# Long convolution and cosine-gated MLP: evictions shared out anew, matrices of two steps made by ScalarE and GpSimd, some made a step earlier

## The chip, the cores and the metric

The kernel runs on one core of a Trainium2 chip. The metric is the device time of one execution in microseconds (us), where lower is better. Kernels are compared by fast runs, and all runs of this study were fast. A difference under 2% counts as "same". All differences here but one (e11) are below that mark, so I give 95% intervals.

PE is TensorE's matmuls, PEld its weight loads, DVE VectorE, ACT ScalarE, POOL GpSimd, SP (or SPq) SyncE, which issues the transfers. An eviction is the copy of a matmul's result out of PSUM (where the matmuls of this kernel write) into SBUF (where its other tiles lie).

## The reference

```
# x, v: (4, 12480, 128)
h_filt = relu(pos_emb @ w1) @ w2 * exp(-0.01 * pos)      # the filter
y = irfft(rfft(x*v, 2S) * rfft(h_filt, 2S))[:S]          # long convolution
z = (x * y).reshape(49920, 128)
h = z @ w_in                                             # 128 -> 2048
out = (h * cos(h)) @ w_out                               # 2048 -> 128
```

## The kernel before

The convolution is done as a transform in two factors (96 and 120) with matmuls. For batch 0 the stages come one after the other: u = x·v and the filter, the **first step** (of the filter, then of the data), the **second step** with the product in frequency, the **third step**, and the **last step**, which runs beside the first blocks of the MLP. The matrices of the second step (w) and the last step (tm) are made on the chip for batch 0 and stored in DRAM; the other batches load them. All later convolution work is interleaved with the MLP.

Every such matrix is a sum of two scaled rows. This helper makes one:

```
def turn(dst, first, second, one, other, half=None, spare=None):
    term = dst
    if half is not None:
        term = half()[...]                       # a PSUM bank
    nc.scalar.activation(term, first, AF.Copy, scale=one)              # ScalarE
    if spare is None:
        nc.vector.scalar_tensor_tensor(out=dst, in0=second, scalar=other, in1=term,
                                       op0=ALU.mult, op1=ALU.add)      # VectorE
    else:
        nc.gpsimd.tensor_scalar(out=spare, in0=second, scalar1=other, ...)
        nc.gpsimd.tensor_tensor(dst, term, spare, op=ALU.add)
```

The second step (48 iterations, two matrices each) has two buffers for w and for h, both stored by SyncE in program order (h is the filter after its second step):

```
with tc.tile_pool(name="both", bufs=2) as pool:
    def before(j):
        ws[j] = pool.tile([KE, 2, N2], F32, name="w")
        for i in range(2):
            make_w(ws[j][:, i, :], 2 * j + i, half=bank)
        nc.sync.dma_start(wd[j, :, :, :], ws[j][:, :, :])
    ...
    def after(j, ps):
        h = pool.tile([N2, 2, 2, D], F32, name="h")
        nc.scalar.activation(h..., ps[1][0:N2, :], AF.Copy, scale=1.0 / M)
        nc.sync.dma_start(hd[j, :, :, :, :], h[:, :, :, :])
        yield from f2_product(pool, ps[0], h, 2 * j)   # VectorE products, GpSimd sums
```

The last step of batch 0 makes four matrices for each of 30 groups, three by VectorE and one by GpSimd, with one spare buffer (`bufs=1`). Beside it run the u multiplies and sums of batch 1, and the MLP, whose step per 128 hidden features is this chain over four engines:

```
ph = w_in.T @ at                      # PE
a  = ph / (2 pi) + 0.25               # ScalarE
k  = (a + ROUND) - ROUND              # VectorE
f  = a - k                            # GpSimd
cs = sin(2 pi f)                      # ScalarE, one step later
gt = ph * cs                          # VectorE
acc += w_out.T @ gt                   # PE
```

## Time and profile before

The median is 3817.88 us over four runs (3814.89 to 3822.04). The profiled execution has a span of 3819.3 us.

| engine | busy share of the span |
|---|---|
| PE | 97% |
| VectorE | 73% |
| GpSimd | 67% |
| ScalarE | 65% |

These shares average a long stretch in which PE is full with a short beginning in which it isn't. Only the beginning can give something back. The borders of its stages are marks in the trace: the first matmul of a step, the first transposes of the MLP, and the 30 results "zs" of the last step.

| stage of batch 0 | us before |
|---|---|
| u, filter, first steps: until the second step's first matmul | 182.4 |
| second step | 106.6 (its h instructions 2.14 apart) |
| third step | 59.8 |
| start of the last step, until the MLP's first transposes | 19.4 |
| from there to the last zs, 617.6 | 249.4 (its zs 9.07 apart) |

### The profile page before, as it was taken

What the parts mean: (1) busy time and instruction counts of PE and PEld (TensorE: products, weight loads), DVE (VectorE), ACT (ScalarE), POOL (GpSimd) and SP (SyncE); (2) the same over time, 40 slices, a digit from 0 to 9 for tenths busy, and PEclk for the clock granted to TensorE, in tenths of its full rate; (3) what the DMA queues carried; (4) which work ended last, traced back from release to release, by engine and by line L of the source; (5) the groups of instructions that cost most, each with busy time, mean ns of one, the idle gap of its engine ahead of it and who ended that gap; (6) DMA issues with size and microseconds to landing.
All of it is one profiled execution on the core that took longest, in us unless ns stands there. A gap on an engine that the chain in (4) does not pass through costs nothing.

```text
span 3819.3 us, 47226 instructions
## 1 busy us (share of the span) xinstructions
PE 3713.3 (97%) x13546; PEld 2117.3 (55%) x13546; DVE 2804.5 (73%) x5737; ACT 2488.4 (65%) x4597; POOL 2559.8 (67%) x2307
## 2 busy tenths in 40 slices
PE   7797989999999999999999999999999999999999
PEld 6777545655566555545566556555566544444444
DVE  7796898678876787787766787787765566666666
ACT  5654666766665556766655567666664677777777
POOL 6564776478854665588845664788644577777776
PEclk9898999999999999999999999999999999999999
DMA  6163442022201651122203640222105200000000
GB/s 164 49 174 93 134 144 79 12 72 78 77 25 29 188 175 30 31 75 78 68 12 96 182 131 12 57 75 77 49 18 164 83 17 22 18 17 23 17 17 17
DMA packets 209082, 274.65 MB, mean 72 GB/s; under 512 B 17062, under 2 KB 146486, under 8 KB 208694
## 3 DMA queue, kind: packets, MB, share of 16 engines
q1 hardware_dynamic: 208822, 271.63, 24.5%
q8 instruction: 109, 1.79, 0.2%
q14 instruction: 151, 1.24, 0.1%
HBM read 191.93 MB, written 79.63 MB: 71 GB/s over the span
## 4 chain that ended last, share of the span: by engine, by line
PE 85%; DVE 5%; POOL 3%; DMA 3%; ACT 2%; issue 2%; SPq 0%; DVEq 0%; POOLq 0%; ACTq 0%
PE ph L691 32%; PE acc L716 28%; PE cv L716 5%; PE cv L482 5%; PE cv L457 4%; PE cv L394 3%; PE cv L433 3%; PE ph L126 2%; POOL f L700 2%; DMA hd<-h 2%; PE ps L457 1%; ACT cs L705 1%; DVE k L697 1%; PE ps L394 1%; DVE xt L382 1%
## 5 line engine op out<-in xcount | busy, mean ns | idle before, releaser
L700 POOL TENSOR_TENSOR f<-a,k 128x512 f32<-128x512 f32 x1568 | 1989.4, 1269 | 1070.6 <-DVE k L697 1067.8
L691 PE MATMUL ph<-at,w_in_sb 128*128 128x512 f32 x3136 | 1602.7, 592 | 18.6 <-DVE gt L707 18.2
L694 ACT ACTIVATE a<-ph,quarter 128x512 f32<-128x512 f32 x1568 | 1073.3, 684 | 756.9 <-PE ph L691 747.8
L716 PE MATMUL acc<-gt,w_out_sb 128*128 128x512 f32 x2656 | 1362.4, 594 | 5.5 <-ACT ot L722 5.3
L707 DVE TENSOR_TENSOR gt<-ph,cs 128x512 f32<-128x512 f32 x1568 | 1078.1, 688 | 326.4 <-ACT cs L705 298.2
L697 DVE TENSOR_SCALAR k<-a 128x512 f32<-128x512 f32 x1568 | 781.5, 498 | 599.4 <-ACT a L694 583.6
L705 ACT ACTIVATE cs<-f 128x512 f32<-128x512 f32 x1568 | 980.3, 625 | 363.8 <-POOL f L700 362.2
L716 PEld LDWEIGHTS acc<-gt,w_out_sb 128*128 128x128 f32 x2656 | 500.9, 189 | 651.2 <-issue 614.1
L691 PEld LDWEIGHTS ph<-at,w_in_sb 128*128 128x128 f32 x3136 | 553.9, 190 | 358.3 <-issue 262.9
L452 POOL TENSOR_TENSOR slots<-slots,t 120x256 f32<-120x256 f32 x384 | 310.9, 816 | 63.0 <-DVE t L451 25.8
L482 PEld LDWEIGHTS cv<-slots,tm 96*104 96x104 f32 x1920 | 243.0, 172 | 100.0 <-issue 86.0
L482 PE MATMUL cv<-slots,tm 96*104 96x128 f32 x1920 | 254.6, 275 | 3.8 <-DVE tm L282 3.8
L716 PE MATMUL cv<-gt,w_out_sb 128*128 128x512 f32 (+1 forms) x480 | 238.5, 579 | 1.0 <-DVE gt L707 1.0
L457 PEld LDWEIGHTS cv<-cs,slots 120*96 120x96 f32 x1536 | 176.9, 167 | 69.1 <-issue 68.7
L457 PE MATMUL cv<-cs,slots 120*96 120x120 f32 x1536 | 183.2, 266 | 0.0
L433 PE MATMUL cv<-slots,w 124*120 124x256 f32 x576 | 173.0, 380 | 0.0
L433 PEld LDWEIGHTS cv<-slots,w 124*120 124x120 f32 x576 | 103.3, 184 | 122.4 <-issue 109.4
L394 PEld LDWEIGHTS cv<-c,slots 104*124 104x124 f32 x768 | 132.8, 192 | 63.8 <-issue 58.3
L716 PEld LDWEIGHTS cv<-gt,w_out_sb 128*128 128x128 f32 x480 | 90.9, 190 | 110.2 <-issue 106.9
L394 PE MATMUL cv<-c,slots 104*124 104x192 f32 x768 | 150.4, 326 | 0.0
L382 DVE TENSOR_TENSOR xt<-xt,vt 104x256 f32<-104x256 f32 x200 | 143.0, 717 | 0.7 <-DMA vt<-in_v_dram 0.4
L467 DVE TENSOR_TENSOR slots<-cv,other 96x240 f32<-96x240 f32 x384 | 133.6, 394 | 2.8 <-ACT other L465 2.8
(125 smaller groups left out, 2529.3 us busy)
## 6 DMA issues: line engine op xcount, KB each, us to landing
h<-hd SPq DMA_DIRECT2D x144, 240.0 KB
tm<-td SPq DMA_DIRECT2D x90, 312.0 KB
xt<-in_x_dram SPq DMA_DIRECT2D x120, 208.0 KB
vt<-in_v_dram SPq DMA_DIRECT2D x120, 208.0 KB
xs<-in_x_dram SPq DMA_DIRECT2D x120, 208.0 KB
zd<-zs SPq DMA_DIRECT2D x120, 208.0 KB
zb<-zd SPq DMA_DIRECT2D x97, 256.0 KB
w<-wd SPq DMA_DIRECT2D x144, 116.2 KB
```

Source lines behind the costliest of these rows:

```text
L394: nc.tensor.matmul(ps[0:KE, i * 2 * N1:(i + 1) * 2 * N1], u[:, b, 0:KE, i], c1[0:u.shape[0], :, :].rearrange("p r k -> p (r k)"), start=Tr ...
L433: nc.tensor.matmul(pi, w[:, i, :], parts[0:KE, :, k], start=True, stop=True)
L452: nc.gpsimd.tensor_tensor(y[:, r], y[:, r], t[:, r], op=op)
L457: nc.tensor.matmul(ps[0:N1, (i * 2 + r) * N2:(i * 2 + r + 1) * N2], parts[0:N2, r, :, b, i], cs[:, r, :], start=True, stop=True)
L482: nc.tensor.matmul(ps[0:R, i * D:(i + 1) * D], t[:, i, r, :], slots[0:N1, :, place, :], start=(r == 0), stop=(r == 1))
L691: nc.tensor.matmul(ph[:, 0:m], w_in_sb[:, c * P:(c + 1) * P], ats[n][:, 0:m], start=True, stop=True)
L694: nc.scalar.activation(a[:, 0:m], ph[:, 0:m], AF.Identity, bias=quarter[:, 0:1], scale=INV_TWO_PI)
L697: nc.vector.tensor_scalar(out=k[:, 0:m], in0=a[:, 0:m], scalar1=ROUND, scalar2=ROUND, op0=ALU.add, op1=ALU.subtract)
L700: nc.gpsimd.tensor_tensor(f[:, 0:m], a[:, 0:m], k[:, 0:m], op=ALU.subtract)
L705: nc.scalar.activation(cs[:, 0:m], f[:, 0:m], AF.Sin, scale=TWO_PI)
L707: nc.vector.tensor_tensor(gt[:, 0:m], ph[:, 0:m], cs[:, 0:m], op=ALU.mult)
L716: nc.tensor.matmul(accs[n][:, 0:m], w_out_sb[:, c, :], gt[:, 0:m], start=(c == 0), stop=(c == NFC - 1))
```

## The change

The intent is to take work from VectorE where it is the busiest engine. The first steps give more evictions to ScalarE. In the second step one of the two w of an iteration is made by ScalarE (two scalings) and GpSimd (an add). In the last step two of four matrices are made so, 15 u multiplies go to GpSimd, and six of the 30 groups are made beside the third step and only loaded later. The essential parts of the diff:

```diff
     def turn(...)
-            nc.gpsimd.tensor_scalar(out=spare, in0=second, scalar1=other, scalar2=None,
-                                    op0=ALU.mult)
+            nc.scalar.activation(spare, second, AF.Copy, scale=other)
             nc.gpsimd.tensor_tensor(dst, term, spare, op=ALU.add)
 ... (F1 evictions: f1_takers(b) -> f1_takers(b, share), the share to ScalarE)
-        if b % 2 == 0:
+        if int((b + 1) * share) > int(b * share):
 ... (second step)
-                for i in range(2):
-                    make_w(ws[j][:, i, :], 2 * j + i, half=bank)
+                make_w(ws[j][:, 0, :], 2 * j, half=bank)
+                spare = pool.tile([KE, N2], F32, name="spare")
+                make_w(ws[j][:, 1, :], 2 * j + 1, spare=spare[:, :])
 ... (last step)
+    SOME = range(4, NG, 5)
+    def make_group(pool, g, t, summed, bufs=1):     # `summed` matrices by ScalarE + GpSimd
+        for i, n2 in enumerate(n2s(g)):
+            if i < G - summed:
+                make_t(t[:, i, :, :], n2)
+            else:
+                spare = pool.tile([N1, 2, R], F32, name="spare", bufs=bufs)
+                make_t(t[:, i, :, :], n2, spare=spare[:, :, :])
+            yield
+        nc.sync.dma_start(td[g, :, :, :, :], t[:, :, :, :])
-                if b == 0:
-                    ... (three matrices by VectorE, one with a spare, bufs=1)
+                if b == 0 and j not in SOME:
+                    for _ in make_group(pool, j, ts[j], G // 2):
+                        pass
                 else:
                     nc.sync.dma_start(ts[j][:, :, :, :], td[j, :, :, :, :])
 ... (u of batch 1)
-        new = u_units(b + 1, 3, slots[0:R, :, :, :], lambda j, half: nc.vector,
+        new = u_units(b + 1, 3, slots[0:R, :, :, :],
+                      lambda j, half: nc.gpsimd if b == 0 and j % 2 > half else nc.vector,
 ... (8 u multiplies of batch 0 also to GpSimd; shares 0.53 and 0.57 for the first steps;
      the inverse tables' sines one table later; 3.4 -> 3.5 MLP steps per group in the last step;
      SOME's groups made beside the third step)
```

More of the change, by code (lines that the diff above doesn't have):

```diff
@@ L182, with __init__ @@
     class Tables:
-        def __init__(self, pool, engine):
+        def __init__(self, pool, engine, lag):
             self.pool, self.engine = pool, engine
+            self.lag, self.waiting = lag, []
             self.prod, self.moved = (
@@ L205, in sines @@
             for dst, quarters in outs:
-                turned = self.pool.tile([P, P], F32, name="turned", bufs=2)
+                turned = self.pool.tile([P, P], F32, name="turned", bufs=self.lag + 1)
                 m, t = self.moved[0:p, 0:n], turned[0:p, 0:n]
@@ L217, in sines, with finish @@
                 self.engine.tensor_tensor(t, m, t, op=ALU.subtract)
+                self.waiting.append((dst, t, TWO_PI / turn))
                 yield
-                nc.scalar.activation(dst, t, AF.Sin, scale=TWO_PI / turn)
+                if len(self.waiting) == self.lag:
+                    self.finish(1)
+        def finish(self, n):
+            for _ in range(n):
+                dst, t, scale = self.waiting.pop(0)
+                nc.scalar.activation(dst, t, AF.Sin, scale=scale)
     def forward_tables(pool):
-        t = Tables(pool, nc.vector)
+        t = Tables(pool, nc.vector, 1)
         part = t.whole([P, 1], [[1, 1]], channel_multiplier=1, name="part")
@@ L245, in inverse_tables @@
     def inverse_tables(pool):
-        t = Tables(pool, nc.gpsimd)
+        t = Tables(pool, nc.gpsimd, 2)
         part = t.whole([P, 1], [[1, 1]], channel_multiplier=1, name="part")
@@ L260, in inverse_tables @@
                            eighths=slice(H - 1, N2, H))
+        t.finish(1)
         for kept, made in ((csd, cs), (rowsd, rows), (twd, tw_t)):
@@ L396, in f1_mm, with f1_takers @@
                          start=True, stop=True)
-    def f1_takers(b):
-        if b % 2 == 0:
+    def f1_takers(b, share):
+        if int((b + 1) * share) > int(b * share):
             return nc.scalar.copy, lambda out, in_: nc.scalar.activation(
@@ L404, in f1_takers, with f1_evict @@
             out=out, in0=in_, scalar1=-1.0, scalar2=None, op0=ALU.mult)
-    def f1_evict(ps, b):
-        copy, negated = f1_takers(b)
+    def f1_evict(ps, b, share):
+        copy, negated = f1_takers(b, share)
         pj = ps[:, 0:4 * N1].rearrange("p (i r k) -> p r k i", i=2, r=2)
@@ L413, in f1_evict, with f1_evict_filter @@
         yield
-    def f1_evict_filter(ps, b):
-        copy, negated = f1_takers(b)
+    def f1_evict_filter(ps, b, share):
+        copy, negated = f1_takers(b, share)
         pj = ps[:, 0:4 * N1].rearrange("p (i k) -> p k i", i=2)
@@ L521, in units @@
         yield REST
+    SOME = range(4, NG, 5)
     REST = 3.0
     U_STEPS, F1_STEPS, F2_STEPS, I1_STEPS, I2_STEPS = 2.0, 0.8, 2.9, 0.8, 1.5
-    FIRST_STEPS, I2U_STEPS = 3.4, 3.0
+    FIRST_STEPS, I2U_STEPS = 3.5, 3.0
     def u_units(b, bufs, u, engine, side="left"):
@@ L545, in u_units, with f1_units @@
                              ahead=bufs - 2)
-    def f1_units(bank, u, evict=f1_evict):
+    def f1_units(bank, u, share=0.5, evict=f1_evict):
         def mm(j, ps, i):
@@ L552, in mm @@
             return ps
-        return units(CB, F1_STEPS, lambda j: None, mm, lambda j, ps: evict(ps, j), 2)
+        return units(CB, F1_STEPS, lambda j: None, mm, lambda j, ps: evict(ps, j, share), 2)
     def f2_units(bank):
@@ L611, in i1_units, with some_groups @@
                              lambda j, ps: i1_evict(pool, ps, j), 2)
+    def make_group(pool, g, t, summed, bufs=1):
[7 more added lines that the diff above has]
+        nc.sync.dma_start(td[g, :, :, :, :], t[:, :, :, :])
+    def some_groups(pool):
+        for g in SOME:
+            t = pool.tile([N1, G, 2, R], F32, name="some", bufs=2)
+            yield from make_group(pool, g, t, G, bufs=2)
     def i2_units(bank, b, bufs):
@@ L619, in before @@
                 ts[j] = pool.tile([N1, G, 2, R], F32, name="tm", bufs=bufs)
-                if b == 0:
-                    for i in range(G):
-                        if i < G - 1:
-                            make_t(ts[j][:, i, :, :], n2s(j)[i])
-                        else:
-                            spare = pool.tile([N1, 2, R], F32, name="spare", bufs=1)
-                            make_t(ts[j][:, i, :, :], n2s(j)[i], spare=spare[:, :, :])
-                    nc.sync.dma_start(td[j, :, :, :, :], ts[j][:, :, :, :])
+                if b == 0 and j not in SOME:
+                    for _ in make_group(pool, j, ts[j], G // 2):
+                        pass
                 else:
@@ L772 @@
                 first_u = u_units(0, 3, slots[0:R, :, :, :],
-                                  lambda j, half: nc.vector if half and j % 3 else nc.gpsimd)
+                                  lambda j, half: nc.vector if half and j % 3 and j < 18
+                                  else nc.gpsimd)
                 next(first_u)
@@ L802 @@
                         next(first_u)
-            f1 = f1_units(bank, ftile[0:FR, :, :, :], f1_evict_filter)
+            f1 = f1_units(bank, ftile[0:FR, :, :, :], 0.53, f1_evict_filter)
             for _ in first_u:
@@ L813, with beside @@
                     pass
-            def beside(units, pieces, bufs):
-                with tc.tile_pool(name="convert", bufs=bufs) as pool:
-                    convert = convert_units(pool, pieces)
+            def beside(units, pieces, more=lambda pool: iter(())):
+                with tc.tile_pool(name="convert", bufs=1) as pool:
+                    convert, other = convert_units(pool, pieces), more(pool)
                     for i, _ in enumerate(units):
@@ L822, in beside @@
                             next(convert, None)
-                    for _ in convert:
-                        pass
-            beside(f1_units(bank, slots[0:R, :, :, :]), [(wind[:, c], w) for c, w in in_pieces], 1)
+                        elif i % 5 == 0:
+                            next(other, None)
+                    for _ in [*convert, *other]:
+                        pass
+            beside(f1_units(bank, slots[0:R, :, :, :], 0.57),
+                   [(wind[:, c], w) for c, w in in_pieces])
             lpool = ctx.enter_context(tc.tile_pool(name="late", bufs=1))
@@ L842 @@
             nc.sync.dma_start(w_in_sb[:, :], wind[:, :])
-            beside(i1_units(bank), [(w_out_sb[:, c, :], w) for c, w in out_pieces], 1)
+            beside(i1_units(bank), [(w_out_sb[:, c, :], w) for c, w in out_pieces], some_groups)
         ps_acc = ctx.enter_context(tc.tile_pool(name="ps_acc", bufs=1, space=PSUM))
```

## The prediction

> **What bounds the kernel now.** I first read the page's row of 40 slices, to see where TensorE (PE) is not full.
>
> ```profile
> PE   7797989999999999999999999999999999999999
> DVE  7796898678876787787766787787765566666666
> ```
>
> Only the first seven slices (some 640 us) have room on PE. After them PE is full, and the work it does there is not changed, so anything won or lost before 640 us moves the end one for one. I then cut that stretch by the program's loops and asked for the busy time of each engine in each (columns: PE, weight loads, VectorE, ScalarE, GpSimd, granted clock, DMA share, GB/s):
>
> ```profile
> 63.00:98.00 35.00, 31.48 (x164) 29.87 (x164) 30.92 (x99) 20.88 (x92) 23.21 (x30) 0.89 0.49 140
> 98.00:126.00 28.00, 22.78 (x101) 20.64 (x102) 22.37 (x85) 18.42 (x79) 20.64 (x52) 0.76 0.05 14
> 126.00:182.00 56.00, 43.07 (x249) 41.70 (x247) 46.34 (x122) 39.91 (x118) 28.59 (x32) 0.95 0.20 57
> 182.00:289.00 107.00, 97.24 (x481) 74.33 (x481) 92.55 (x288) 52.91 (x138) 67.58 (x96) 0.98 0.58 168
> 289.00:349.00 60.00, 56.21 (x514) 55.72 (x515) 49.74 (x155) 28.72 (x86) 30.61 (x37) 0.95 0.17 55
> 380.00:640.00 260.00, 236.69 (x851) 128.13 (x852) 232.91 (x387) 160.97 (x314) 192.96 (x179) 0.96 0.44 130
> ```
>
> 63 to 126 is the filter's first step (after 98 beside the sine tables), 126 to 182 the data's first step (beside the conversion of w_in), 182 to 289 the second step, 289 to 349 the third, 380 to 640 the last step of batch 0 beside the MLP. VectorE looks like the limit in most, and the change relieves VectorE. The waits and the timeline say that this is only part of it.
>
> Data's first step: VectorE's conversion instruction waits for a store of the conversion (timeline of VectorE; the brackets give the idle time before it).
>
> ```profile
> 147.39 0.29 DVE L133 TENSOR_SCALAR power<-raw 128x256 uint32<-128x256 uint32 x1 [2.29 <-DMA wind<-power]
> ...
> 160.06 0.29 DVE L133 TENSOR_SCALAR power<-raw 128x256 uint32<-128x256 uint32 x1 [1.42 <-DMA wind<-power]
> ```
>
> Six of the eight pieces show this wait; their GpSimd parts start 6.1 to 7.1 us apart, from 134.58 to 173.02. The loop is GpSimd 1.08 + 1.08 + 0.73 + 0.73, store 1.9 to 2.8, VectorE 0.3, plus hand-overs.
>
> Second step: the chain is a ring through the two buffers of h.
>
> ```profile
> 201.35 0.60 ACT h L595
> 201.94 0.34 ACT ps L280 x2
> 202.28 3.22 DMA hd<-h
> ...
> 205.61 0.60 ACT h L595
> 206.21 0.46 ACT ps L280 x2
> 206.67 3.84 DMA hd<-h
> ```
>
> The "ps L280" pieces are not ScalarE holding up the store. The store of h is issued by SyncE behind the store of the next matrix w, and SyncE waits for w to be made:
>
> ```profile
> SPq L584 <- DVE w L282: 63.1, 46, 3.4
> ```
>
> Last step of batch 0: VectorE is 90% busy (232.91/260), but part of that is waiting: GpSimd's f and VectorE's k exclude each other.
>
> ```profile
> 449.13 1.27 POOL L700 TENSOR_TENSOR f<-a,k 128x512 f32<-128x512 f32 x1 [0.36 <-DVE k L697]
> ...
> 449.58 1.10 DVE L697 TENSOR_SCALAR k<-a 128x512 f32<-128x512 f32 x1
> ...
> 452.24 0.41 DVE L697 TENSOR_SCALAR k<-a 128x512 f32<-128x512 f32 x1
> ```
>
> **What the Trainium skill says.** "SBUF — State Buffer", Who interferes with whom: VectorE and GpSimd share a port pair, held for a whole instruction against two-port modes or two SBUF inputs. The trace agrees: k is 0.41 us alone, 1.10 beside f. "GPSIMD Engine Reference", 1. Specifications: GpSimd has no PSUM access. Hence half of w must now be scaled into SBUF, not a PSUM bank. "ScalarE: Activation LUTs", What ACT_TABLE_LOAD costs: 186 ns + 93 for a pointer operand + 0.833 ns per element, neighbours overlapping by 93. For 208 elements that is 452; the trace has 456, four in 1.54 us, so one costs about 0.38 in a row. "DMA: Bandwidth & Descriptors", Anatomy of one DMA: about 2.0 us fixed per transfer, mostly completion (a fit for GpSimd-issued ones). The 3.2 us of a 240 KB store agree in kind: the ring is latency.
>
> **The change, part by part.**
>
> *Filter's first step.* int(64 x 0.53) = 33 blocks instead of 32 go to ScalarE: VectorE saves one block of 0.45 + 0.24 + 0.36 + 2 x 0.25 = 1.56 us. Eight u multiplies (of the last 12 u blocks, those with j%3 not 0) move from VectorE (0.50) to GpSimd (0.72 to 0.95), so VectorE saves 4 us. A u block took (99.04 - 63.84)/12 = 2.93 us; now GpSimd has 2 x 0.86 + 0.98 = 2.7 and hand-overs, so GpSimd becomes its limit and about 0.2 x 12 = 2.5 us are won. The first table sine held ScalarE 11.0 us, because GpSimd was still at u until 100. Lag 2 puts that sine 2.5 blocks later, some 1.4 us of ScalarE work, but the 22.9 us of table work on GpSimd (100.09 to 122.97) still follow u and the last sine must still be done. I take -3 us for both.
>
> *Data's first step.* int(64 x 0.57) = 36 blocks go to ScalarE; VectorE loses four of 1.23 = 5 us. But six of eight intervals are the conversion loop, which keeps its length; VectorE just waits longer there. Only the nine blocks after the last wait gain, about one VectorE block: -1 us.
>
> *Second step.* Per iteration VectorE loses one 0.33 us instruction of some 1.95 us. ScalarE gets a third scaling (0.3) in an idle gap of 0.9; GpSimd gets an add of 124x120 (0.44, as its 96x120 add has) after its two products. Now the ring, with the end of h(j-2) as zero. Before: VectorE's products end at 1.47 and two w at 2.05; store of w issued 2.07, of h(j-1) 0.34 later, 2.41; + 3.2 landing + 0.1 + 0.6 for h(j+1) = 6.3 for three iterations, 2.10 each. Measured: h(0) ends near 186.8, h(47) near 287.3, so 100.4/47 = 2.14. The model holds. After: w waits for GpSimd, whose products end at 2.32 (213.25 to 215.58 in the timeline); + 0.06 + 0.44 for the add + 0.06 + 0.34 = 3.22 for the issue of h(j-1)'s store; + 3.9 = 7.12, so 2.37 each. That is 47 x 0.23 = +11 us; a store that lands a little faster at a lower rate takes 1 off. +10 us: this part makes its stage slower.
>
> *Third step.* Added: 6 groups x 4 matrices x 2 scalings = 48 of 0.38 to 0.46 on ScalarE (18 to 22 us, 28.7 + 22 = 51 of 60) and 24 adds of 0.69 = 17 on GpSimd (31 + 17 = 48 of 60). PE with 512 matmuls at 0.112 = 57 us stays the limit. 0 us.
>
> *Start of the last step.* Groups 0 to 3 wait for two GpSimd adds, not one (a spare pair with one buffer costs about 0.8 more, +2 us on the chain to the first MLP block); group 4 is loaded, not made, so SyncE need not wait 2.3 us for it in front of the store that the second MLP block needs. 0 us.
>
> *Last step of batch 0.* VectorE's matrices fall from 90 to 24 x 2 = 48, and 15 of 60 u multiplies go to GpSimd. Per group before: 263/29 = 9.07 us (results from 354.7 to 617.6). VectorE: 8.3 - 1.4 x 0.51 - 0.5 x 0.64 + 0.1 MLP step x 1.15 = 7.4. GpSimd: 6.8 - 0.9 (one scaling gone) + 0.6 adds x 0.8 + 0.5 x 0.86 + 0.13 = 6.9. ScalarE rises from 62% to some 75%. PE: a group of the second batch takes (1438.2 - 1232.4)/29 = 7.1 us at 3.0 MLP steps, PE full; half a step more at 1.75 makes 8.0. PE could then be the limit, but GpSimd at 87% and VectorE at 92% share the port. Adding GpSimd's time and VectorE's instructions on the shared pair gives 10.9 before (1.2 times 9.07); after, 10.35, by the same 1.2 some 8.6. So 29 x (9.07 + 0.1 x 1.75 - 8.6) = -19 us (the 0.175 is MLP work done earlier, not lost).
>
> Sum: -3 - 1 + 10 + 0 + 0 - 19 = -13 us; 3818.5 - 13 = 3805.
>
> **Rivals.** (1) VectorE is the true limit of every early stage, as its busy share suggests. Then the second step wins 48 x 0.33 = 16, the first steps about 9, and the last step becomes PE-bound (-36): 3757. Against it: the h ring reproduces 2.14 us without it, and the conversion wait is in the trace. (2) The second step is slowed as reckoned, but the last step gains little, because added GpSimd work holds the port that VectorE needs and ScalarE waits for the single spare: 3818 to 3823. For it: k at 1.10 beside f. Against it: GpSimd's total per group hardly grows. (3) The second step is not slowed, GpSimd's add fitting before the store of h is due: 3795. Against it: SyncE's order, in which h's store stands behind w's.
>
> **Range and chances.** The uncertain terms are the second step (0 to +14), the last step (-30 to -5) and the first steps (-8 to 0). Errors partly cancel: 3786 to 3822. A gain of 2% needs 3742, below rival (1), and a loss of 2% needs 76 us that no part adds.
>
> **What would show it.** Right: in the second step h instructions some 2.35 us apart instead of 2.14, SyncE's store of w waiting for GpSimd's add, VectorE's share down to about 70%; conversion pieces still 6 to 7 us apart; groups of the last step about 8.6 us apart; PE full after 640. Wrong: second step under 100 us (rival 1 or 3), last-step groups at 8.0 or still at 9 (rival 1 or 2), a third step over 63 us, or a gap on PE at a later step.

## The result, and the profile after

| | median us | runs | range |
|---|---|---|---|
| before | 3817.88 | 4 | 3814.89 to 3822.04 |
| changed | 3834.97 | 4 | 3831.41 to 3837.92 |

The ratio is 1.0044, with a 95% interval of 1.0026 to 1.0061. A ratio compares the fast runs of the two kernels from the same rounds, so it isn't quite the ratio of the medians. The change makes the kernel some 17 us slower, where 13 us faster was predicted. It is still "same" by the 2% mark, but outside the predicted range. The mean granted TensorE clock was 0.989 before and 0.988 after, which is worth some 4 of these 17 us (an estimate: 0.001 of 3819 us), so the clock isn't the main cause. Within the last step it was 0.93 and 0.92.

The slices of the changed kernel have the same form as before. The second, third, fifth and sixth digits of PE have moved by one, up or down, and from the sixth slice on every digit is a nine.

```profile
PE   7887899999999999999999999999999999999999
DVE  7776787678876787677766887778765566666666
```

The table of stages shows where the time came from (profiled spans 3819.3 and 3834.5, so +15.2 to explain).

| stage | before | after | difference | predicted |
|---|---|---|---|---|
| until the second step | 182.4 | 179.5 | −3 | −4 |
| second step | 106.6 | 117.0 | +10.4 | +10 |
| third step | 59.8 | 63.0 | +3 | 0 |
| start of the last step | 19.4 | 21.3 | +2 | 0 |
| last step, less MLP work done earlier (30 × 0.1 × 1.75 = 5.2) | 249.4 | 252.2 | +3 | −19 |
| sum | | | +15.4 | −13 |

Each column is one profile. The same code gives borders that differ from profile to profile: the second step began between 176.7 and 181.0 in the 16 profiles with the first steps as changed, and between 182.4 and 184.9 in the four with them as before (the means differ by 4.7). The zs were 9.24 to 9.39 apart in the five profiles with the changed last step (changed, e5, e6, e8, e9), and 9.07 and 8.95 in the two with the old one (before, e14; granted clock in the last step 0.93 and 0.95). So in the first steps and the last step 2 to 3 us, or 0.1 us between groups, is no finding. The third step is steadier: 62.1 to 63.5 in all profiles with groups beside it, 58.1 to 59.8 in all without, so its +3 is real.

So one line is badly wrong: the last step lost 3 us instead of winning 19. The busy times of the engines in the stages of the changed kernel (columns: stretch, length, PE, weight loads, VectorE, ScalarE, GpSimd, clock, DMA share, GB/s):

```profile
63.00:123.00 60.00, 52.53 (x266) 49.92 (x267) 51.49 (x173) 40.13 (x176) 48.43 (x89) 0.87 0.30 88
123.00:180.00 57.00, 47.30 (x249) 46.14 (x248) 40.65 (x106) 43.57 (x129) 28.67 (x33) 0.89 0.19 56
180.00:296.00 116.00, 99.99 (x480) 73.20 (x478) 80.27 (x239) 69.30 (x188) 86.32 (x143) 0.99 0.53 154
296.00:358.00 62.00, 56.68 (x512) 55.32 (x512) 49.61 (x151) 41.54 (x129) 43.78 (x59) 0.94 0.25 81
394.00:655.00 261.00, 236.37 (x838) 126.87 (x839) 208.72 (x330) 169.71 (x331) 186.88 (x179) 0.95 0.44 129
```

The third line is the second step: VectorE is busy 80.27/116 = 69%, down from 86%, and the stage takes longer. The last line is the last step: VectorE is at 208.72/261 = 80%, down from 90%, GpSimd at 72% and ScalarE at 65%. PE's share hasn't risen (236.37/261 = 91%, as before), and the groups are 9.39 us apart instead of 9.07. Where an engine has been relieved and nothing became faster, its busy share wasn't the limit. The next thing to read is the waits.

**Data's first step.** The timeline of VectorE shows one of six such waits for the conversion's store; the pieces are 6.1 to 6.5 us apart (139.26, 145.72, 152.18 and so on). This loop kept its length, as predicted.

```profile
152.18 0.29 DVE L133 TENSOR_SCALAR power<-raw 128x256 uint32<-128x256 uint32 x1 [1.72 <-DMA wind<-power]
```

**Second step.** SyncE's waits (columns: total us, times, longest), from 180 to 296:

```profile
SPq L596 <- POOL w L296: 44.2, 47, 1.0
```

SyncE now waits for GpSimd's add in front of every store of w, which the prediction had named. But the engines' waits hold a second thing, which it had not:

```profile
ACT w L290 <- DMA wd<-w: 35.7, 38, 3.4
```

ScalarE writes the first term of the second matrix into w itself, since the term no longer goes to a PSUM bank. So ScalarE must wait until the store of the w before last has left that buffer. The chain of waits through the stage has many rounds like this one (start, duration, what); w's stores make up 34.5% of it, h's 9.0%:

```profile
242.96 0.40 ACT w L290
243.35 0.29 ACT spare L295
...
243.67 0.39 POOL slots L462
244.06 0.41 POOL w L296
...
244.48 2.81 DMA wd<-w
...
247.40 0.40 ACT w L290
```

One round takes 247.40 − 242.96 = 4.44 us and makes two iterations, as there are two buffers, so 2.22 us each. The instructions on h are 2.32 apart on average, so other rounds take longer.

**Last step.** The groups of VectorE from 400 to 600 us (columns: operation, count, busy us, mean ns, idle us before it and what ended it). First the kernel before, then the changed one:

```profile
L697 DVE TENSOR_SCALAR k<-a 128x512 f32<-128x512 f32 x75 | 50.1, 667 | 3.2 <-ACT a L694 3.2
```

```profile
L721 DVE TENSOR_SCALAR k<-a 128x512 f32<-128x512 f32 x73 | 63.2, 866 | 22.5 <-ACT a L718 22.5
```

The MLP's k now takes 866 ns instead of 667, and VectorE stands idle 22.5 us for its input a, not 3.2. The timeline shows how both come about in one group; first ScalarE, then VectorE, then GpSimd:

```profile
471.20 0.47 ACT L295 ACTIVATE spare<-rows,tw_t 96x208 f32<-96x208 f32 x1 [0.61 <-POOL tm L296]
471.57 0.67 ACT L718 ACTIVATE a<-ph,quarter 128x512 f32<-128x512 f32 x1
```

```profile
472.34 1.68 DVE L721 TENSOR_SCALAR k<-a 128x512 f32<-128x512 f32 x1 [0.73 <-ACT a L718]
```

```profile
471.74 0.63 POOL L296 TENSOR_TENSOR tm<-tm,spare 96x208 f32<-96x208 f32 x1 [0.58 <-ACT spare L295]
472.32 0.74 POOL L397 TENSOR_TENSOR slots<-xt 104x256 f32<-104x256 f32 x1
473.00 0.74 POOL L391 TENSOR_TENSOR xt<-xt,vt 104x256 f32<-104x256 f32 x1
474.11 1.27 POOL L724 TENSOR_TENSOR f<-a,k 128x512 f32<-128x512 f32 x1 [0.36 <-DVE k L721]
```

ScalarE's second scaling into the spare waits 0.61 us, because there is one spare buffer and GpSimd is still adding from it; the MLP's next a stands behind it in ScalarE's order. VectorE waits 0.73 for that a. Then k, which takes 0.41 alone, takes 1.68, because GpSimd has begun its u sum 0.02 us before it and goes straight on to the moved u multiply: k ends (474.02) only after that multiply has (473.74). It isn't the only one: between 355 and 640 us ten k's stand beside an add, a u sum and a moved multiply and take 1.67 to 1.69 us, and ten beside an add and a u sum alone, 0.99 to 1.02. The MLP's next f comes after k. So there are two suspects: the wait for the spare, and the u multiplies on GpSimd.

### The profile page after: what moved, and what is told of

It is laid out like the page before. It is cut to its first block, busy times and chain, and to the rows that moved or that the text cites. A ratio compares the mean times of both kernels' runs of the same rounds, so it can differ in the third digit from the quotient of the medians.

```text
span 3834.5 us, 47433 instructions
## 1 busy us (share of the span) xinstructions
PE 3723.5 (97%) x13546; PEld 2120.4 (55%) x13546; DVE 2759.8 (72%) x5607; ACT 2534.9 (66%) x4734; POOL 2590.6 (68%) x2390
## 4 chain that ended last, share of the span: by engine, by line
PE 83%; POOL 5%; ACT 4%; DVE 4%; DMA 3%; issue 2%; SPq 0%; DVEq 0%; POOLq 0%; ACTq 0%
PE ph L715 32%; PE acc L740 27%; PE cv L740 5%; PE cv L492 5%; PE cv L467 4%; PE cv L443 3%; PE cv L403 3%; POOL f L724 2%; PE ph L126 2%; DVE k L721 1%; DMA wd<-w 1%; PE ps L467 1%; ACT cs L729 1%; ACT tm L290 1%; ACT spare L295 1%
## 5 line engine op out<-in xcount | busy, mean ns | idle before, releaser
L715 PE MATMUL ph<-at,w_in_sb 128*128 128x512 f32 x3136 | 1605.0, 593 | 20.3 <-DVE gt L731 19.4
L721 DVE TENSOR_SCALAR k<-a 128x512 f32<-128x512 f32 x1568 | 792.2, 505 | 625.4 <-ACT a L718 607.6
L391 DVE TENSOR_TENSOR xt<-xt,vt 104x256 f32<-104x256 f32 x177 | 130.0, 736 | 0.1
```

The lines of the kernel that those rows point to most:

```text
L715: nc.tensor.matmul(ph[:, 0:m], w_in_sb[:, c * P:(c + 1) * P], ats[n][:, 0:m], start=True, stop=True)
L721: nc.vector.tensor_scalar(out=k[:, 0:m], in0=a[:, 0:m], scalar1=ROUND, scalar2=ROUND, op0=ALU.add, op1=ALU.subtract)
```

## The experiments

All 18 runs gave correct results, so that isn't repeated. "Against before" is (ratio − 1) × 3818; the changed kernel stands at +17 (+10 to +23 by its own interval, as it had four runs). The column "apart" is the mean distance of the zs of the last step, or of h where the experiment is about the second step, each from one profile.

| kernel | median us | ratio [95%] | against before, us | apart, us |
|---|---|---|---|---|
| changed | 3834.97 | 1.0044 [1.0026, 1.0061] | +17 | zs 9.39, h 2.32 |
| e1_spare2 | 3822.80 | 1.0007 [1.0000, 1.0014] | +3 | zs 8.92 |
| e2_one | 3817.92 | 0.9997 [0.9988, 1.0005] | −1 | zs 8.99 |
| e3_spread | 3839.03 | 1.0053 [1.0038, 1.0068] | +20 | zs 9.48 |
| e4_u_vec | 3823.96 | 1.0011 [1.0004, 1.0018] | +4 | zs 9.03 |
| e5_w_old | 3823.50 | 1.0012 [1.0006, 1.0019] | +5 | h 2.15, zs 9.37 |
| e6_apart | 3831.84 | 1.0036 [1.0024, 1.0049] | +14 | h 2.34 |
| e7_no_some | 3840.42 | 1.0055 [1.0038, 1.0072] | +21 | zs 9.67 |
| e8_h_first | 3854.14 | 1.0093 [1.0078, 1.0108] | +36 | h 2.75 |
| e9_apart_h_first | 3831.68 | 1.0030 [1.0018, 1.0042] | +11 | h 2.26 |
| e10_spare2_u | 3817.81 | 0.9998 [0.9989, 1.0006] | −1 | zs 8.89 |
| e11_lag2 | 3949.90 | 1.0341 [1.0325, 1.0356] | +130 | zs 9.65 |
| e12_best | 3810.45 | 0.9976 [0.9967, 0.9985] | −9 | zs 8.90 |
| e14_first_only | 3812.83 | 0.9984 [0.9978, 0.9991] | −6 | zs 8.95 |
| e15_u_gpsimd | 3823.72 | 1.0010 [1.0002, 1.0019] | +4 | zs 9.03 |
| e16_memset | 3820.65 | 1.0005 [0.9997, 1.0014] | +2 | zs 8.99 |
| e17_best_one | 3802.64 | 0.9960 [0.9947, 0.9972] | −15 | zs 8.66 |
| e18_idle_mult | 3827.03 | 1.0021 [1.0012, 1.0030] | +8 | zs 9.23 |
| e19_one_no_some | 3810.82 | 0.9979 [0.9971, 0.9986] | −8 | zs 8.92 |

### The last step: the spare, the number of matrices, the burst, the u multiplies

**e1_spare2**: the changed kernel with a second spare buffer, nothing else.

```diff
-                    for _ in make_group(pool, j, ts[j], G // 2):
+                    for _ in make_group(pool, j, ts[j], G // 2, bufs=2):
```

> The changed kernel with two spare buffers instead of one for the groups made in the last step. Theory B (ScalarE takes its orders in a row: the six scalings of a group, and its wait for GpSimd's add to free the one spare, stand between two activations of the MLP): the wait of ScalarE for the spare, 13.2 us between 400 and 640 us in the changed kernel, goes; groups of the last step 9.39 us apart fall to 8.8 to 9.1, the kernel gains 8 to 15 us on the changed one (about 3822 us). Theory P (the port shared by VectorE and GpSimd is the limit, as the prediction reckoned): nothing moves, 9.3 to 9.4.

Measured: +3 instead of +17, zs 8.92 apart. The waits of the changed kernel between 400 and 640 us hold these two lines:

```profile
DVE k L721 <- ACT a L718: 29.5, 37, 2.3
...
ACT spare L295 <- POOL tm L296: 13.2, 19, 1.2
```

With two spares, between 400 and 625, the second line is gone and the first is a third:

```profile
DVE k L721 <- ACT a L718: 9.7, 15, 1.3
```

Beside the u multiplies on GpSimd, the single spare costs some 14 us of the whole time, about what ScalarE waits for it.

**e2_one**: the changed kernel with one matrix of a group by ScalarE and GpSimd and three by VectorE, as before.

```diff
-                    for _ in make_group(pool, j, ts[j], G // 2):
+                    for _ in make_group(pool, j, ts[j], 1):
```

> The changed kernel with one matrix of four, not two, made by ScalarE and GpSimd in the last step; VectorE adds the other three, as before the change. Theory B: five scalings in a row and no wait for the spare, so the burst shrinks from 2.9 us to 1.9; groups fall to about 8.5 to 8.8 us apart, 15 us gained on the changed kernel. Theory V (VectorE's own work is the limit): 24 adds of 0.56 us come back, groups 9.7 apart, 10 us lost. Theory P: GpSimd loses 24 adds of 0.76, VectorE gains as many of 0.56: little, 3 us gained.

Measured: −1, zs 8.99 apart. VectorE has one instruction more in each group, and the kernel is 18 us faster. So the VectorE instruction that the change removed wasn't worth what replaced it. (The edit also ends the wait for the spare, which by e1 is 14 of these 18. The profile, with 8.99, is of the slowest of its 12 runs.)

**e3_spread**: the same matrices with the same single spare, made in two bursts with the group's first matmuls between them, to see whether the length of the burst on ScalarE's queue is what hurts.

```diff
-                    for _ in make_group(pool, j, ts[j], G // 2):
-                        pass
+                    rest[j] = make_group(pool, j, ts[j], G // 2)
+                    for _ in range(G + 1 if j == 0 else G // 2):
+                        next(rest[j], None)
 ... (in mm, when the group before has its second half)
+                    for _ in rest.pop(j + 1, ()):
+                        pass
```

> The changed kernel with the same work for a group of the last step, but two matrices made where all four were, and the other two half a group (1.75 MLP steps) later. No instruction added or removed. Theory B: bursts half as long, absorbed by the buffers of the MLP; groups 8.5 to 8.9 us apart, 12 to 20 us gained on the changed kernel. Theories P and V (sums of work on the port or on VectorE): no change, 9.3 to 9.5.

Measured: +20, zs 9.48 apart, no better than the changed kernel. ScalarE still waits 11.8 us for the spare. So the length of the burst isn't what hurts; by e1 it is the wait in it.

**e4_u_vec**: the changed kernel with batch 1's u multiplies all on VectorE again, with the single spare.

```diff
-                      lambda j, half: nc.gpsimd if b == 0 and j % 2 > half else nc.vector,
+                      lambda j, half: nc.vector,
```

> The changed kernel with the u multiplies of the last step all on VectorE, as before the change. Theory V: 15 multiplies of about 0.62 us come back to VectorE, groups 9.6 to 9.7 apart, 6 to 9 us lost. Theory P: GpSimd loses 15 of about 0.86: 2 to 4 us gained. Theory B: neither is on the loop through ScalarE, within 3 us of the changed kernel.

Measured: +4, zs 9.03 apart: a gain of some 13 us from giving VectorE 15 instructions back. None of my theories had expected that much. In the trace the k's beside a moved multiply (1.67 to 1.69 us) are gone: the 20 k's beside an add and a u sum take 0.99 to 1.07. This run, more than any other, turned the search to the port that VectorE and GpSimd share.

**e10_spare2_u**: e1 and e4 together.

> The changed kernel with both cures of the last step: two spare buffers, and the u multiplies of the last step on VectorE. Alone they gained 13 and 12 us. If both shorten the same loop (GpSimd's instructions in front of f, ScalarE waiting behind them), they add up only in part: 15 to 20 us gained, groups of the last step 8.6 to 8.8 us apart, near PE's own 8.0. If they act on different limits, 25 us and 8.1 to 8.3. If VectorE takes over as the limit, no more than one of them alone: 12 us, 9.0.

Measured: −1, zs 8.89 apart: 18 us better than the changed kernel. The two single gains, 14 and 13, don't add. With two spares the u multiplies on GpSimd cost only about 3 to 5 more (+3 against −1; medians 3822.80 and 3817.81). And without them the single spare costs only some 5 (e4, +4, against −1). Why they don't add isn't shown. The multiplies don't lengthen ScalarE's wait for the spare: it is 13.0 us in e4 and 13.2 in the changed kernel. What e4 shortens is VectorE's wait for a, from 29.5 us to 21.0.

### What a multiply on GpSimd costs

Three kernels take the kernel before and add one thing to its last step.

**e15_u_gpsimd**: only the 15 u multiplies moved to GpSimd.

```diff
-        new = u_units(b + 1, 3, slots[0:R, :, :, :], lambda j, half: nc.vector,
+        new = u_units(b + 1, 3, slots[0:R, :, :, :],
+                      lambda j, half: nc.gpsimd if b == 0 and j % 2 > half else nc.vector,
```

> The kernel before with the last step's part for u alone: 15 of its 60 multiplies go from VectorE to GpSimd. Order theory (each stands on GpSimd in front of an f, and f is on the loop that sets the MLP's pace): 15 x 0.72 = 11 us slower, less what VectorE gains, so 6 to 12 us slower than before, 3825 to 3832. Theory of busy engines (VectorE 90%, GpSimd 74% busy in that stage before): 5 to 9 us faster, 3811 to 3815.

Measured: +4. The groups of VectorE, 400 to 600 us, of before (its k is shown above) and of this kernel:

```profile
L382 DVE TENSOR_TENSOR xt<-xt,vt 104x256 f32<-104x256 f32 x44 | 27.4, 622 | 0.0
L388 DVE TENSOR_TENSOR slots<-xt 104x256 f32<-104x256 f32 x22 | 21.0, 956 | 0.0
```

```profile
L698 DVE TENSOR_SCALAR k<-a 128x512 f32<-128x512 f32 x75 | 53.0, 707 | 1.8 <-ACT a L695 1.8
...
L388 DVE TENSOR_TENSOR slots<-xt 104x256 f32<-104x256 f32 x22 | 24.3, 1103 | 0.0
L382 DVE TENSOR_TENSOR xt<-xt,vt 104x256 f32<-104x256 f32 x33 | 23.2, 703 | 0.0
```

Eleven multiplies fewer at 0.622 should save 6.8 us of VectorE in this window. But the k are 2.9 us longer, the u sums 3.3, and the 33 multiplies that stayed 33 × 0.081 = 2.7: together 8.9. VectorE's busy time in the window rose from 182.0 to 183.7. Moving the instruction relieved nothing. The zs are 9.03 apart, no more than before (9.07), so the profile doesn't show where the 4 us (+1 to +7) were lost.

**e16_memset** and **e18_idle_mult** leave all u multiplies on VectorE and add 15 idle instructions to GpSimd at the places where the change puts its multiplies: a memset, which reads nothing, or a multiply of a scratch tile with itself.

```diff
+        idle = mpool.tile([R, BANK], F32, name="idle", bufs=1) if b == 0 else None
+        def taker(j, half):
+            if b == 0 and j % 2 > half:
+                nc.gpsimd.memset(idle[:, :], 0.0)                  # e16_memset
+                nc.gpsimd.tensor_tensor(i, i, i, op=ALU.mult)      # or e18_idle_mult
+            return nc.vector
```

> The kernel before with 15 idle memsets of 104x512 (0.53 us each, into a tile nobody reads) on GpSimd, where the changed kernel has its u multiplies; VectorE keeps the multiplies. Nothing waits for them and they wait for nothing. Order theory: 15 x 0.53 = 8 us slower than before, 3827. Port theory (a GpSimd instruction costs VectorE time only if it reads SBUF): within 3 us of before, 3817 to 3822. Theory of the wait for the vt load: within 3 us too.

> The kernel before with 15 idle multiplies of 104x256 (0.72 us each, reading and writing a tile nobody else uses) on GpSimd in the place of the 15 memsets; VectorE keeps all u multiplies. Port theory: each keeps VectorE from the port for up to 0.72 us, 15 x 0.72 = 11 us at most, so 5 to 11 us slower than before, 3824 to 3831. Theory of the multiply's place in the u chain: nobody waits for these, so as the memsets, 0 to 2 us slower.

Measured: the 15 memsets (0.52 us each in the trace) cost +2, with an interval that holds zero; the 15 multiplies (0.72 us each expected, 0.90 on average in the trace) cost +8 (+5 to +11). GpSimd's place in the order of work is the same in both, but the multiplies keep it longer, by 15 × 0.38 = 5.7 us, about the difference in cost. So the times alone don't exclude a longer GpSimd queue as the reason; a memset as long as the multiply wasn't tried. The durations on VectorE say more (355 to 640 us). Its multiply xt takes 0.41 us beside a memset in 11 of 11 cases, as it does alone, and 0.72 on average in the 8 beside an idle multiply alone. So for xt it matters that the multiply reads SBUF. k is held up by both: 0.83 us in the two cases beside an idle multiply alone, and 2.03 to 2.05 in the three that stand beside f, a u sum and a memset, where the one beside f and a u sum takes 1.58. On average over 400 to 600 us k takes 700 ns in e18, against 667 before and 680 in e14, which has the same last step as before:

```profile
L708 DVE TENSOR_SCALAR k<-a 128x512 f32<-128x512 f32 x71 | 49.7, 700 | 5.2 <-ACT a L705 5.2
```

An idle GpSimd multiply thus cost 8/15 = 0.53 us of the end time, where it ran for 0.90. Against e18 (+8), e15 (+4) also takes 15 multiplies off VectorE, so these are worth some 4 us (the intervals overlap), less than GpSimd's multiplies cost.

### The second step

**e5_w_old**: the changed kernel with the second step as before.

```diff
-                make_w(ws[j][:, 0, :], 2 * j, half=bank)
-                spare = pool.tile([KE, N2], F32, name="spare")
-                make_w(ws[j][:, 1, :], 2 * j + 1, spare=spare[:, :])
+                for i in range(2):
+                    make_w(ws[j][:, i, :], 2 * j + i, half=bank)
```

> The changed kernel with the second step's matrices made as before the change (both halves by ScalarE into PSUM and VectorE). If the second step's part costs what the stage borders say (178.6 to 296.5 against 182.0 to 289.0), h instructions are 2.14 us apart again instead of 2.32, and the kernel gains 8 to 11 us on the changed one: 3824 to 3827 us. If that part pays elsewhere what it costs here, the total stays at 3835.

Measured: +5, h 2.15 apart. That part of the change costs 12 us, where 10 was predicted.

**e6_apart**: ScalarE scales into a tile of its own, so that only GpSimd's add writes to w. The edit also takes the second buffer from the spare.

```diff
-                spare = pool.tile([KE, N2], F32, name="spare")
+                spare = pool.tile([KE, N2], F32, name="spare", bufs=1)
+                apart = pool.tile([KE, N2], F32, name="apart", bufs=1)
-                make_w(ws[j][:, 1, :], 2 * j + 1, spare=spare[:, :])
+                make_w(ws[j][:, 1, :], 2 * j + 1, spare=spare[:, :], apart=apart[:, :])
```

> The changed kernel; in the second step ScalarE scales into a tile of its own instead of into w, so that ScalarE never waits for the store of the w before last; GpSimd adds into w. Theory W (what slows the second step is ScalarE waiting for the store of w, 35.7 us in all, with h in line behind it): h instructions fall from 2.32 us apart to 2.05 to 2.2, 6 to 12 us gained on the changed kernel. Theory S (the prediction's: SyncE issues h's store behind w's, which waits for GpSimd's add): they stay at 2.3 to 2.4.

Measured: +14, h 2.34 apart. The wait of 35.7 us for w's store is gone, and the stage isn't faster. The chain is now the ring of h that the prediction had worked out:

```profile
225.54 0.47 POOL w L296
...
226.04 0.33 ACT apart L290
226.36 3.11 DMA hd<-h
...
229.57 0.61 ACT h L608
```

One round, from an h (222.71) to this one, is 6.86 us for three iterations, 2.29 each. (The scaling into "apart" is only what ScalarE ended while SyncE was issuing the two stores; the add of w is what released them.) Two rings had nearly the same length, and to cut one only uncovered the other. (ScalarE also waits 9.2 us, 23 times, for GpSimd's add to free the single "apart"; in the round shown that isn't on the chain.)

**e8_h_first**: the store of h issued in front of that of a later w.

```diff
                 nc.sync.dma_start(hd[j, :, :, :, :], h[:, :, :, :])
+                if j + 2 < N1 // 2:
+                    nc.sync.dma_start(wd[j + 2, :, :, :], ws[j + 2][:, :, :])
 ... (and no store of w in `before` for j >= 2)
```

> The changed kernel with the order of SyncE's two stores in the second step turned round: h's store first, w's after it, nothing else moved. Theory S: h's store starts about 0.9 us earlier, h instructions 2.1 to 2.2 us apart instead of 2.32, 5 to 10 us gained on the changed kernel. Theory W: w's store is no earlier, so no change or slightly slower, 2.3 to 2.4.

Measured: +36, h 2.75 apart, worse than expected. The store of w now leaves later, and ScalarE waits 47 us in all for it: two starts of that store in the chain, 218.33 and 223.86, are 5.53 us apart for two iterations, 2.76 each. That confirms that w's two buffers are a ring of their own; I had misjudged how much later the store would leave.

**e9_apart_h_first**: e6 and e8 together.

> The changed kernel with both edits of the second step at once: ScalarE scales into a tile of its own, and h's store goes ahead of w's. Alone the first gave 2.34 us between h instructions, the second 2.75. If there are two rings, one through w's store and ScalarE, one through h's store behind w's on SyncE, both are open now and h's own ring (0.6 + 0.35 + 3.2 + 0.1 for two iterations) is left: 2.1 to 2.2, 8 us gained on the changed kernel. If the GpSimd add itself is the limit: still 2.3.

Measured: +11, h 2.26 apart, still not 2.14. Now VectorE's write of the first w waits for w's store (19.2 us in 26 waits) and ScalarE's scaling for GpSimd's add (35.5 us in 44). All three variants leave some ring of about 2.3 us or more. That w is finished by GpSimd after its product sums is common to them and may be the reason, but that isn't shown: e6 and e9 had one buffer each for apart and spare, two weren't tried.

### The other parts, and a version that beats both

**e7_no_some**: no groups made beside the third step (`SOME = ()`).

> The changed kernel with no group made beside the third step; all thirty are made in the last step, two matrices each by ScalarE and GpSimd. The third step should be as short as before (about 59 us instead of 61.5) and the start of the last step as well; but six more groups then pay the wait for the single spare and the scalings. Loop theory (what stands in ScalarE's and GpSimd's order between f and the next a adds to the MLP one for one): groups about 9.5 apart instead of 9.39, the whole within 4 us of the changed kernel, on either side. If making a fifth beside the third step was worth what it intended: 6 x 2.5 = 15 us slower.

Measured: +21, zs 9.67 apart, but the third step is 4 us shorter (57.1 against 61.1 from its first matmul to its last copy). Making a fifth of the matrices early is worth about 4 us net here, and the two intervals (+14 to +27 and +10 to +23) overlap. It isn't free, as I had thought: it gives the third step's 4 us up for the last step's 8.

**e14_first_only**: the kernel before with only the first steps' parts of the change.

> The kernel before with the first steps' parts of the change alone (0.53 and 0.57 of the evictions on ScalarE, the sines' lag of 2, the late u multiplies on GpSimd); second, third and last step as before. The prediction gave -4 us; the stage borders of the changed kernel give -3. Expected 3815 to 3817 us. If the shifts of evictions are hidden behind the conversion's stores and the tables: no change, 3819.

Measured: −6 (−3 to −8). A bit more than the −4 predicted, which is within the interval.

**e11_lag2**: the changed kernel with the MLP's sine and gating two steps after a, k and f instead of one, to give the loop from f over cs to the next a, k and f some slack.

```diff
-            if 0 <= i - 1 < len(steps):
-                gates[i - 1] = moe_act(mpool, *hidden.pop(i - 1))
+            if 0 <= i - 2 < len(steps):
+                gates[i - 2] = moe_act(mpool, *hidden.pop(i - 2))
 ... (and three buffers for f)
```

> The changed kernel with cs and gt of the MLP taken two steps after a, k and f instead of one (three buffers for f); no instruction more or less, and the engines' sums the same. Loop theory: the loop f, cs, a, k, f then spans three steps instead of two, so that the extra scalings and the wait for the spare have slack; groups of the last step fall from 9.39 us apart to 8.2 to 8.7, 15 to 30 us gained on the changed kernel. Theories of a full engine or of the shared port: no change, 9.3 to 9.4.

Measured: +130. This misfired: each ph stays a step longer in one of four PSUM buffers, and PE then waits for gt even in the MLP alone at the end (480 of 500 us busy between 3000 and 3500, where it was 500). It says nothing about the loop, and I could not test the loop in another way.

**e12_best**: the changed kernel with e1, e4 and e5.

> The changed kernel with two spare buffers, u multiplies of the last step on VectorE, and the second step as before the change. If the parts add up: 17 us from the first two (as measured together) and 11.5 from the second step (as measured alone), so 3806 to 3808 us, 12 us faster than before the change. If the second step's gain is eaten by a later start of the rest: 3818.

Measured: −9 (−5 to −13).

**e17_best_one**: the changed kernel with e2, e4 and e5, so: first steps and the fifth beside the third step as changed, one matrix of a group by ScalarE and GpSimd, u on VectorE, the second step as before.

> The best version so far (3810), but with one matrix of a group by ScalarE and GpSimd and three by VectorE in the last step, instead of two and two with a second spare buffer. With one, two and two's replacement gained 16 us on the changed kernel, against 13 for the second buffer; if that holds here, 3806 to 3809. If VectorE, which gets 24 adds of 0.56 us back on top of the u multiplies, becomes the limit: 3815 to 3820.

Measured: −15 (−11 to −20), 3802.64 us, zs 8.66 apart. It beats both kernels, though by 0.4% only. Its profiled run is the fastest of its five, at a clock of 0.992. Beside the changed kernel's, the third and fifth digits of its slices are nines again, while the second and the sixth stay above those of before:

```profile
PE   7897999999999999999999999999999999999999
```

**e19_one_no_some**: e17 without groups beside the third step.

> The best version (3802.6) with no group made beside the third step. In the changed kernel the fifth was worth 5.4 us (3840.4 against 3835.0). If it is worth the same here: 3808. If the last step, no longer held up by the single spare, takes six more groups for less: 3803 to 3805.

Measured: −8. The fifth beside the third step is worth 7 us in the best version.

## Why the prediction was wrong

**What held.** *First steps*: −4 predicted, −3 by the borders of one pair of profiles, −4.7 by the means of all and −6 alone (e14). The conversion loop kept its length, as said; how much relief it hid wasn't measured apart. *Second step*: +10 predicted, +10.4 by the borders and 12 by e5. So rivals (1) and (3), which let it gain or stay, are refuted. The mechanism was half right. The predicted ring of h, with SyncE's store behind w's, exists and has about the predicted length (2.29 measured in a round of e6, 2.37 predicted). But in the changed kernel another ring of nearly the same length (2.22 in the round shown) binds more often: ScalarE writes into w and so waits for w's store. The prediction had seen that the second term must go to SBUF, and not that the first now goes into w itself. After 640 us PE is full, as predicted.

**The step that failed** is the last term, "29 x (9.07 + 0.1 x 1.75 - 8.6) = -19 us". It measured +3, and this 22 us is most of the miss of 30. In particular it is the sentence "Adding GpSimd's time and VectorE's instructions on the shared pair gives 10.9 before (1.2 times 9.07); after, 10.35, by the same 1.2 some 8.6". It scales a sum of busy times by one ratio found at one point. Three things in it were wrong:

1. *The wait for the single spare wasn't in it.* The prediction counted this wait in the start of the last step and in rival (2), and left it out of the groups, where it comes up again and again. It costs 14 us (e1) beside the moved multiplies and 5 without them (e4 against e10), as ScalarE's next a, and with it k and f, stand behind it.
2. *The u multiplies were counted as relief.* The sum took 0.5 × 0.64 us of each group from VectorE and added 0.5 × 0.86 to GpSimd, which leaves the total nearly unchanged. In the runs GpSimd's multiplies held up VectorE's k, sums and multiplies by more than they took away (8.9 against 6.8 us in e15's window): alone the move cost 4 us (e15), and beside the single spare 13 (e4). An idle multiply cost 0.53 us each (e18), a memset hardly anything (e16).
3. *A second matrix per group is no gain.* With two spares and u on VectorE, going from two such matrices to one brings zs from 8.90 to 8.66 apart and the time from −9 to −15 (e12, e17). ScalarE's two scalings and GpSimd's add cost more than VectorE's one instruction. The two intervals overlap a little; e1 against e2 (+3 and −1, with the u multiplies on GpSimd) points the same way.

In group distances, points 1 and 2 together are 9.39 − 8.89 = 0.50 us (e10) and point 3 is 8.90 − 8.66 = 0.24, so 0.74 of the 0.79 by which 8.6 was missed. That is a rough sum, as each distance is from one profile. The version that undoes these parts comes to 8.66, but by another division of the work, so it is luck that this is near the predicted 8.6.

**The terms given as 0.** The third step lost 3 and the start 2. PE's 57 us was taken as the limit of the third step, but e7 shows that the added work there costs 4 us, and with 63.0 the step stands at the "over 63" that was to show the prediction wrong. The start's +2 for two adds through a single spare was worked out and then cancelled against a shorter wait of SyncE; it came all the same. The three profiles with two spares have starts of 20.1 to 21.0 (e1, e10, e12) instead of 21.3, so the spare explains half of it or less.

**The rivals.** Rival (2) named both causes, the port and the single spare, and was set aside because "GpSimd's total per group hardly grows". The total wasn't what counted: in the trace the cost lay in k's held up and in waits for the spare. Its own figure, 3818 to 3823, was too low as well, since it let the last step gain a little. The range then had its upper end at 3822, because no term was allowed to fall on the losing side except the second step.

**What stays open.** What bounds the best version at 8.66 us per group, where PE's own work is 8.0 by the prediction's estimate, isn't settled. I think that the limit is the loop from f over cs and a to k, which in two steps takes about PE's own 3.5 us and so has no slack for scalings between; e11 was to test that and failed for another reason. That the effects of the spare and the multiplies don't add fits such a loop, but is no proof of it. Part of the differences in the last step goes with the granted clock: it was 0.92 in the changed kernel and 0.95 in e1 and e17, and for the same 895 matmuls PE was busy 239.3, 232.0 and 229.1 us. Whether the clock follows from PE's gaps or comes on top of them, no run here shows.

## What to carry to other kernels

An engine with the highest busy share may be busy because it is held up: before moving its instructions to the neighbour that holds it up, put the same instruction idle on that neighbour and see what it costs. When a producer changes from a scratch buffer to the final buffer, ask which store must have left that buffer: a pair of buffers with a 2.8 us store is a ring with its own period. A helper that one engine fills and another empties needs two buffers as soon as it is used twice in a row, above all where the filling engine has the critical chain's next instruction behind it.

## What the Trainium skill lacked or had wrong

- "SBUF — State Buffer", Who interferes with whom, says that a VectorE instruction with two SBUF inputs contends with a GpSimd instruction that reads SBUF, not with one that only writes it. The runs agree for xt: 0.41 us beside a memset, 0.72 beside an idle multiply. What no page has is the size of the effect when work is shared out ("Perfetto Trace Analysis", Optimizing Scalar/DVE Operations, only warns that such a move might not help): moving 15 multiplies from VectorE to GpSimd left VectorE's busy time in the window at 183.7 us, where it was 182.0, and made the kernel 4 us slower (e15).
- "Perfetto Trace Analysis", Identifying the Most-Contended Engine, says to take the engine with the highest occupancy and optimize it first, and calls occupancy a fair measure for VectorE. With PE judged by its weight loads (128.13/260 = 49%), one of the two measures that the page asks for, that was VectorE with 90% in the last step here; the change brought it to 80%, and the groups went from 9.07 to 9.39 us. Part of its occupancy was time in which an instruction was held up (k 0.41 us alone, 1.10 beside f before the change, up to 1.69 after it), which no wait in the trace shows.
- I found no page that tells of a store's completion as the period of a ring of two output buffers: ScalarE waited 35.7 us in 38 waits in the second step for w's stores, most of which took 2.8 to 2.9 us in the chain.
